# Splitting the second pair of each group's weight units one to three steps later in a fused attention and mixture-of-experts kernel

## The chip, the cores and the metric

The kernel runs on one core of a Trainium2 chip. The metric is device time in microseconds (us) for one launch, as the median of several runs; a single profiled execution gives the trace. Engines are named as the profile does: PE is TensorE (the matrix unit), PEld its weight loads, DVE VectorE, ACT ScalarE, POOL GpSimd, and SP is SyncE, which here issues all DMA transfers.

## The reference, cut to what matters

```
# attention, batch 4, heads 8, sequence 576, head size 64
scores = q @ k.T / 8 + (cum[:, None] - cum[None, :])   # cum = cumsum(log f)
scores = where(causal, -1e9, scores)
x = softmax(scores) @ v                   # reshaped to 2304 tokens x 512
# four experts over all tokens, hidden size 1024
p = probs / (probs.sum(-1) + 1e-9)
for e in range(4):
    out += p[:, e] * (maximum(x @ w1[e], 0) @ w2[e])
```

## The kernel before, in words

Attention and experts are interleaved so that PE always has something to multiply. Tokens come in chunks of 256. The expert weights are cut into 32 *units* of 128 x 1024 (a unit is one 128-wide slice of the hidden size: half of it belongs to `w1`, half to `w2`), and the tokens are swept twice, so there are 64 units: 0 to 31 in the first sweep, 32 to 63 in the second. Before PE can use a unit, its fp32 values are *split* into a high and a low half of lower precision, and every product is made of three matmuls (high x high, high x low, low x high).

**A step** is one chunk of tokens with one pair of units. `l1` (L1012, 24 matmuls) makes the hidden values, `gate` makes their high part `gh` on ACT (L1025) and their low part `gl` on DVE (L1026), and `l2` (L1045, 12 matmuls) of the step before multiplies by the second weights; DVE then adds the result to the chunk's sum `acc` (L1072). Two pairs of units (`ps` 0 and 1) are one group; the steps of a group go over the same chunks with both pairs.

**A unit's split** is `w_split(n)`. `w_load` issues the load of the raw unit into a tile `wr` (L937, 512 KB; three buffers). In the second sweep one half of the columns is split by ACT (L979, high part) and DVE (L980, low part), the other by POOL (L971 scales in place), ACT (L974) and POOL again (L975). The result is a pair tile; even units take a slot of the tag `wh`, odd units one of `wl`, with six slots each, and a new unit waits until PE has last used the unit that had its slot. Two steps later SP stores the split unit to memory (`wd`, L988), since a last stage reads it again. When a pair has been used for the last time (`ends` says at which step), the main loop calls `w_split(w0 + 6)` and `w_split(w0 + 7)`, and then `first_units(w0)`.

**The last stage** combines two units at a time (Strassen's scheme) from about 613 us on. Its first tiles are made early: for `w0` in `EARLY = (54, 58)`, `first_units` calls `split_1`, which loads a raw half unit (L1182, `wr64_0`, into the same three `wr` buffers), loads stored units into `bw0` (L1197), has POOL form sums `wt0` (L1177, four instructions that read `wr64_0`) and ACT and POOL split those into `bs0` (L1204, L1208, L1209). Both `bw0` and `bs0` take slots of the tag `wh`. The tiles `bv` (L1239) are further reads of stored units.

**Attention** has its own tiles in between: `raw` is a loaded block of q and k, `q`, `kl`, `hi` (L563, L571, L577, POOL) and ACT's `hi` (L562) prepare it, PE makes the scores (L615), DVE and ACT the softmax (L629, L644), ACT and DVE its normalised halves `z` (L713, L714). SP turns `z` around by DMA transposes into `pt` (L723, three for one half of a head pair), and PE multiplies `pt` with `v` (L816, tile `o`). The names end in head pair, batch and half: `pt3_3_1_1` is batch 3, pair of heads 1, second half, and `z`, `kl`, `q` of that half are made for it.

**What sets the order.** The body writes its instructions in program order, and a scheduler with a model of the engines then fixes the order on each engine, with the program order as the priority. Slots of a tag are handed out in program order too. On SP this order is also that in which DMAs are issued: an issue that waits holds all issues behind it.

Of the kernel before, what the change touches and what calls it, by code (L numbers as in the profile page):

```python
# [25 lines left out]
SWEEPS = (  # L26
    ((0,), (0,), (0, 1), (0, 1, 2)),
    ((1, 2, 3, 4), (1, 2, 3, 4), (2, 3, 4), (3, 4)),
)
# [7 lines left out]
LAST = (5, 6, 7, 8)  # L37
EARLY = (54, 58)
AHEAD = 4
W_SLOT = (4, 6)  # L40
NEAR = 2
JOBS = ((0, 0), (1, 0), (2, 0), (3, 0), (0, 1), (1, 1), (2, 1), (3, 1))
# [36 lines left out]
def fused(ctx: ExitStack, tc: tile.TileContext, qk, v, f, probs, w, out):  # L79
# [110 lines left out]
    def at_step(n, f):  # L190
        later.setdefault(n, []).append(f)
# [47 lines left out]
    def behind(f):  # L239
        if prev is None:  # L240
            f()
            return
        with tc.issue_after(prev.last.ins):
            f()
# [32 lines left out]
    def w_peek(e, i):  # L277

        n, k = divmod(i, 2)
        t = pk_p.tile([128, 512], F32, tag="pk", name=f"pk{e}_{i}")  # L280
        nc.sync.dma_start(out=t, in_=w[8 * e + n, :, 512 * k : 512 * k + 512])
        at_step(
            step + 2,
            lambda: nc.vector.tensor_reduce(
                out=wmax[:, k, n, e : e + 1], in_=t, op=ALU.max, axis=AX.X, apply_absolute_value=True
            ),
        )
# [57 lines left out]
    def v_peek(i):  # L345

        t = xf_p.tile([128, 1024], F32, tag=f"xf{2 + i % 2}", name=f"vp{i}")
        flat = v.rearrange("b r p t h d -> (b r p t h d)").rearrange(
            "(n p f) -> n p f", n=NV, p=128
        )  # L350
        nc.sync.dma_start(out=t, in_=flat[i])

        def top():
            with tc.issue_after(prev.first.ins):
                nc.scalar.activation(
                    out=t,
                    in_=t,
                    func=AF.Abs,
                    scale=1 / 1024,
                    accum_out=vmax[:, i : i + 1],  # L360
                )

        at_step(step + 2, top)
# [570 lines left out]
    def w_load(n):  # L934
        if n < NS and n not in wraw:
            wraw[n] = wr_p.tile([128, 1024], F32, tag="wr", name=f"wr{n}")
            nc.sync.dma_start(out=wraw[n], in_=w[n % 32])  # L937
# [3 lines left out]
    def w_pair(name):  # L941
        t = w_p.tile([128, 2, 1024], F16, tag=("wh", "wl")[len(pairs) % 2], name=name)
        pairs.append(t)
        return t

    def w_split(n):
        w_load(n)
        r = wraw.pop(n)
        if n < 32:
            wh[n] = w_p.tile([128, 1024], F32R, tag="wh", name=f"wh{n}")  # L950
            wl[n] = w_p.tile([128, 1024], F32R, tag="wl", name=f"wl{n}")
            nc.scalar.activation(out=wh[n], in_=r, func=AF.Copy)  # L952
            eng = nc.vector if n in W_DVE else nc.gpsimd
            for a in (0, 512):
                z = a + 512
                eng.tensor_tensor(  # L956
                    out=wl[n][:, a:z],
                    in0=r[:, a:z],
                    in1=wh[n][:, a:z].bitcast(F32),
                    op=ALU.subtract,  # L960
                )
        else:
            e = n % 32 // 8
            assert ("w", e) in known
            t = w_pair(f"w{n}")
            wh[n], wl[n] = t[:, 0], t[:, 1]
            for k in range(2):
                c = slice(512 * k, 512 * k + 512)
                sc = wsc[:, e, k : k + 1]
                if k == 1:  # L970
                    nc.gpsimd.tensor_scalar(  # L971
                        out=r[:, c], in0=r[:, c], scalar1=sc, scalar2=None, op0=ALU.mult
                    )
                    nc.scalar.activation(out=wh[n][:, c], in_=r[:, c], func=AF.Copy)  # L974
                    nc.gpsimd.tensor_tensor(  # L975
                        out=wl[n][:, c], in0=r[:, c], in1=wh[n][:, c], op=ALU.subtract
                    )
                    continue
                nc.scalar.activation(out=wh[n][:, c], in_=r[:, c], func=AF.Copy, scale=sc)  # L979
                nc.vector.scalar_tensor_tensor(  # L980
                    out=wl[n][:, c],
                    in0=r[:, c],
                    scalar=sc,
                    in1=wh[n][:, c],
                    op0=ALU.mult,
                    op1=ALU.subtract,
                )
            at_step(step + 2, lambda: nc.sync.dma_start(out=wd[n - 32], in_=t))  # L988
        w_load(n + 1)
        w_load(n + 2)  # L990
        w_load(n + 3)
# [196 lines left out]
    def split_1(p):  # L1188
        if p >= 16:
            return ()  # L1190
        r = raw_half(p, 0)
        t, u = (
            w_p.tile([128, 2, 1024], F16, tag="wh", name=f"b{k}{p}") for k in ("w", "s")
        )
        one = t.rearrange("p n (s f) -> p n s f", s=2)
        for n in range(2):
            nc.sync.dma_start(out=one[:, n], in_=wd[2 * p + n][:, :, :512])  # L1197
        bw[p] = one, u.rearrange("p s (k f) -> p s k f", k=4)
        f = sums(f"wt{p}", r, SUMS)
        hi, lo = u[:, 0], u[:, 1]  # L1200

        def scale(a):
            x = f[:, a : a + 512]
            nc.scalar.activation(out=x, in_=x, func=AF.Copy, scale=wsc[:, p // 4, 0:1])  # L1204

        def part(a):
            x, h = f[:, a : a + 512], hi[:, a : a + 512]
            nc.scalar.activation(out=h, in_=x, func=AF.Copy)  # L1208
            nc.gpsimd.tensor_tensor(out=lo[:, a : a + 512], in0=x, in1=h, op=ALU.subtract)  # L1209

        return (
            lambda: scale(0),
            lambda: (part(0), scale(512)),
            lambda: part(512),
        )

    def first_units(w0):
        if w0 in EARLY:
            for f_ in split_1(EARLY.index(w0)):
                f_()  # L1220
# [322 lines left out]
    goals = sorted((max(n - LEAD, 1), cost[need[c]]) for c, n in first.items() if n > 0)  # L1543
    goals.append((len(steps) - AHEAD, cost[-1]))
    while goals:
# [17 lines left out]
    def startup():  # L1563
# [13 lines left out]
        for s in range(FIRST + 2):  # L1577
# [24 lines left out]
            if s >= 5 and s % 2 == 1:  # L1602
                heads[s - 4][0].fin()
            if s in W_SLOT:
                w_split(W_SLOT.index(s))

# [9 lines left out]
    j.begin(0)  # L1616
    for n in range(len(W_SLOT), 6):
        w_split(n)

    used = set()  # L1620
    for n in range(len(steps) + 1):
        step = n
        cur = steps[n] if n < len(steps) else None
        for f_ in later.pop(n, ()):
            behind(f_)
        for e, first_ in enumerate(PEEK):
            if 0 <= n - first_ < 16:
                w_peek(e, n - first_)
            if n == first_ + 17:
                a_, b_ = w_scale(e)  # L1630
                behind(a_)
                at_step(n + 3, b_)
        if 0 <= n - V_PEEK < NV:
            v_peek(n - V_PEEK)
        if n == V_PEEK + NV + 1:
            a_, b_ = v_scale()
            behind(a_)
            at_step(n + 2, b_)
        if cur is not None:
            if cur.c not in used:  # L1640
                used.add(cur.c)
                upto(need[cur.c])
            for c, m in TURN:
                if n >= m and c not in yh and ("x", c) in known:
                    narrow(c)
            if cur.s == 1:
                assert cur.c in yh
                weigh(cur.g // 2, cur.c)
            for q in range(4):
                cur.l1(q)  # L1650
                pace(n + q / 8)
            cur.gate()
        else:
            upto(len(asteps))
            chunks.close()
            late.h = late.enter_context(tc.tile_pool(name="h", bufs=4, side="right"))
            for e in range(E):
                weigh(e, LAST[0])
            big = [Big(p) for p in range(16)]
            turns = in_turns(0)  # L1660
            for _ in range(3):
                next(turns)()
        if prev is not None:
            for q in range(4):
                prev.l2(q)
                pace(n + (q + 4) / 8)
                if cur is None:
                    for _ in range(2 if q == 3 else 1):
                        next(turns)()
            for w0, t in ends.items():  # L1670
                if t is prev:
                    if w0 + 7 < NS:
                        w_split(w0 + 6)
                        w_split(w0 + 7)
                    first_units(w0)
        prev = cur

    for p in range(2):
# [88 lines left out]
```

## Time and profile before

| what | value |
| --- | --- |
| median of 3 runs | 942.64 us (941.62 to 944.03) |
| profiled execution: time, span | 939.25 us, 937.5 us |
| mean granted clock of TensorE | 0.985 of full speed |
| busy: PE, DVE, ACT, POOL | 885.3, 709.3, 568.9, 525.1 us |
| moved by DMA | 159.45 MB, mean 170 GB/s |

The profiled execution is 3.39 us (0.4%) below the median of the runs. Its span is the time from its first instruction to its last, and 1.75 us lie around it. All times in the trace count from the span's start.

### The profile page before, as it was taken

Reading aid. Unit: us, or ns where it says so; the run is one execution under the profiler, and the core shown is the slowest. Engines: PE = TensorE matmul, PEld = TensorE weight load, DVE = VectorE, ACT = ScalarE, POOL = GpSimd, SP = SyncE. Lnnn points to the kernel's source line nnn. Section 1 sums busy time; section 2 is a strip of 40 time slices with the busy share of each in tenths; the row PEclk is TensorE's granted clock in tenths of the full one; section 3 lists DMA queues with packets and bytes.
Section 4 is the critical chain, followed back from the end, with each engine's and each line's share of the span. In section 5 each row is a group of like instructions: output and inputs, shape, how many; then the busy total and the mean of one; then the engine's idle time right before and its main releaser. Section 6 shows DMA issues by size and latency. Waiting matters only on the chain. (4 is left out here: it accounts for less than half of the span.)

```text
span 937.5 us, 16657 instructions
## 1 busy us (share of the span) xinstructions
PE 885.3 (94%) x5783; PEld 620.8 (66%) x5783; DVE 709.3 (76%) x1458; ACT 568.9 (61%) x1137; POOL 525.1 (56%) x528
## 2 busy tenths in 40 slices
PE   4899998999998889999999989999998999999998
PEld 3699988999765556666666656654455664666547
DVE  5768665786888988789878887576778757786487
ACT  5869755465676778668666777355665345653350
POOL 4657865478533754327641684265778627785060
PEclk9999999999998988999999999999999999999999
DMA  7458844538879698988999699524322424232003
GB/s 264 146 176 295 291 126 164 186 119 313 227 189 198 152 293 195 311 156 212 306 288 158 119 328 236 135 67 142 129 91 81 145 68 125 79 107 74 23 1 91
DMA packets 147508, 159.45 MB, mean 170 GB/s; under 512 B 86148, under 2 KB 107328, under 8 KB 147424
## 3 DMA queue, kind: packets, MB, share of 16 engines
q1 hardware_dynamic: 147424, 158.39, 60.2%
q8 instruction: 45, 0.74, 0.3%
q14 instruction: 39, 0.32, 0.2%
HBM read 117.30 MB, written 21.65 MB: 148 GB/s over the span
## 5 line engine op out<-in xcount | busy, mean ns | idle before, releaser
L1012 PE MATMUL l<-y,w 128*128 128x256 f16 x1248 | 155.7, 275 | 0.0
L1012 PEld LDWEIGHTS <-w 128*128 128x128 f16 x1248 | 118.3, 99 | 30.6 <-issue 6.5
L644 ACT ACTIVATE p<-p,nm 128x576 f32<-128x576 f32 (+3 forms) x160 | 95.6, 598 | 52.4 <-DVE nm L629 43.5
L1045 PE MATMUL l<-w,gh 128*128 128x512 f16 x408 | 122.6, 383 | 4.8 <-DVE acc L1072 4.8
L714 DVE SCALAR_TENSOR_TENSOR z<-p,rs,z 128x384 f16<-128x384 f32 (+3 forms) x128 | 85.7, 694 | 12.6 <-ACT z L713 11.1
L1072 DVE SCALAR_TENSOR_TENSOR acc<-y,scg,acc 128x256 f32<-128x256 f32 (+1 forms) x164 | 81.1, 515 | 14.9 <-PE y L1283 14.7
L615 PE MATMUL s<-hi 128*128 128x384 f32 (+1 forms) x192 | 76.9, 406 | 16.1 <-DVE hi L577 8.9
L563 POOL CAST q<-raw 64x320 fp32r<-64x320 f32 (+1 forms) x56 | 26.0, 465 | 117.9 <-PE s L615 71.3
L1283 PE MATMUL m<-rh,bs 128*128 128x512 f16 x256 | 86.4, 379 | 0.0
L629 DVE CUSTOM_DVE_ANT_0 p<-s,mask 128x288 f32<-128x288 f32 (+2 forms) x160 | 74.8, 475 | 12.9 <-PE s L615 11.8
L571 POOL TENSOR_TENSOR kl<-raw,hi 64x576 fp32r<-64x576 f32 (+1 forms) x56 | 66.4, 1186 | 28.6 <-ACT hi L562 28.2
L1045 PE MATMUL l<-w,gl 128*128 128x512 f16 x204 | 77.1, 383 | 5.0 <-DVE gl L1026 5.0
L1209 POOL TENSOR_TENSOR bs<-wt,bs 128x512 f16<-128x512 f32 x32 | 38.4, 1201 | 75.7 <-ACT bs L1208 75.4
L971 POOL TENSOR_SCALAR wr<-wr,wsc 128x512 f32<-128x512 f32 x32 | 53.9, 1687 | 35.1 <-DMA wr<-in_w 25.5
L956 POOL TENSOR_TENSOR wl<-wr,wh 128x512 fp32r<-128x512 f32 x48 | 64.4, 1370 | 15.9 <-ACT wh L952 11.6
L713 ACT ACTIVATE z<-p,rs 128x384 f16<-128x384 f32 (+3 forms) x128 | 69.5, 589 | 4.6 <-issue 1.2
L1026 DVE SCALAR_TENSOR_TENSOR gl<-l,gh 128x512 f16<-128x512 f32 (+1 forms) x80 | 54.7, 684 | 19.1 <-ACT gh L1025 18.6
L1012 PE MATMUL l<-xh,wh 128*128 128x256 f32 x224 | 65.0, 292 | 0.8 <-ACT xh L857 0.8
L615 PE MATMUL s<-kl,q 66*128 66x384 f32 (+1 forms) x192 | 63.7, 336 | 2.2 <-DMA kl<-nc 2.2
L1283 PE MATMUL m<-rh,bw 128*128 128x512 f16 x191 | 64.4, 379 | 1.4 <-ACT r L1329 1.4
L1012 PE MATMUL l<-xl,wh 128*128 128x256 f32 x224 | 65.2, 291 | 0.0
L1045 PEld LDWEIGHTS <-gh 128*128 128x128 f16 x408 | 37.0, 98 | 42.2 <-issue 11.2
(387 smaller groups left out, 2359.6 us busy)
## 6 DMA issues: line engine op xcount, KB each, us to landing
wr<-in_w SPq DMA_DIRECT2D x90, 512.0 KB
pk<-in_w SPq DMA_DIRECT2D x64, 256.0 KB
wd<-w SPq DMA_DIRECT2D x32, 512.0 KB
raw<-in_qk SPq DMA_DIRECT2D x32, 448.0 KB
bw<-wd SPq DMA_DIRECT2D x32, 256.0 KB
bv<-wd SPq DMA_DIRECT2D x32, 256.0 KB
raw<-in_qk SPq DMA_DIRECT2D x24, 256.0 KB
vp<-in_v SPq DMA_DIRECT2D x10, 512.0 KB
```

The source lines that it names most:

```text
L571: eng.tensor_tensor(out=kl[:64, :wk], in0=r[:64, ko : ko + wk], in1=hi[:64, ko : ko + wk].bitcast(F32), op=ALU.subtract,)
L615: nc.tensor.matmul(out=ps[:, at : at + z - a], lhsT=lhsT, rhs=rhs, start=(m == 0), stop=(m == 1),)
L629: nc.vector.tensor_tensor_reduce(out=pt[:, a:z], in0=ps, in1=mask[:, m0 + a : m0 + z], scale=-0.125, scalar=BIG if n == 0 else nm[:, col : ...
L644: nc.scalar.activation(out=pt[:, :w_], in_=pt[:, :w_], func=AF.Exp, scale=-1.0, bias=self.nmax[hh][:, c : c + 1], accum_out=self.ssum[:, h ...
L713: nc.scalar.activation(out=o[:, 0], in_=x, func=AF.Copy, scale=sc)
L714: nc.vector.scalar_tensor_tensor(out=o[:, 1], in0=x, scalar=sc, in1=o[:, 0], op0=ALU.mult, op1=ALU.subtract)
L956: eng.tensor_tensor(out=wl[n][:, a:z], in0=r[:, a:z], in1=wh[n][:, a:z].bitcast(F32), op=ALU.subtract,)
L1012: nc.tensor.matmul(out=self.l1p[:, fi, :], lhsT=lhsT, rhs=rhs[:, k, :], start=(k == 0 and m == 0), stop=(k == 3 and m == 2),)
L1026: self.last = nc.vector.scalar_tensor_tensor(out=self.gl, in0=self.l1p, scalar=0.0, in1=self.gh.bitcast(F32) if wide else self.gh, op0=ALU ...
L1045: matmul(out=l2[tt], lhsT=lhsT, rhs=rhs, start=(self.ps == 0 and fi == 0 and m == 0), stop=(self.ps == 1 and fi == 1 and m == 2),)
L1072: nc.vector.scalar_tensor_tensor(out=acc[c][:, tt, d0:d1], in0=ps, scalar=sc, in1=acc[c][:, tt, d0:d1], op0=ALU.mult, op1=ALU.add,)
L1283: line.append(nc.tensor.matmul(**args))
```

## The change

`REST`, indexed by the number of chunks that a group's steps go over, gives a delay in steps: none for one chunk, 1, 2 and 3 steps for two, three and four chunks. For the second pair of a group (`ps` = 1) the two `w_split` calls no longer come at the end of that pair's last step, but `REST[...]` steps later; they are kept in `splits` and called at the end of the loop body, behind `first_units`.

```diff
--- before.py
+++ after.py
@@ -37,6 +37,7 @@
 LAST = (5, 6, 7, 8)
 EARLY = (54, 58)
 AHEAD = 4
+REST = (0, 0, 1, 2, 3)
 W_SLOT = (4, 6)
 NEAR = 2
 JOBS = ((0, 0), (1, 0), (2, 0), (3, 0), (0, 1), (1, 1), (2, 1), (3, 1))
@@ -1617,7 +1618,7 @@
     for n in range(len(W_SLOT), 6):
         w_split(n)
 
-    used = set()
+    used, splits = set(), {}
     for n in range(len(steps) + 1):
         step = n
         cur = steps[n] if n < len(steps) else None
@@ -1670,9 +1671,11 @@
             for w0, t in ends.items():
                 if t is prev:
                     if w0 + 7 < NS:
-                        w_split(w0 + 6)
-                        w_split(w0 + 7)
+                        wait = REST[len(SWEEPS[t.s][t.g // 2])] if t.ps else 0
+                        splits.setdefault(n + wait, []).extend((w0 + 6, w0 + 7))
                     first_units(w0)
+            for m in splits.pop(n, ()):
+                w_split(m)
         prev = cur
 
     for p in range(2):
```

Nine pairs move in the program: units 24 and 25 and units 28 and 29 by one step; 32, 33 and 36, 37 by two; 44, 45 and 48, 49 and 52, 53 by three; 56, 57 and 60, 61 by two. The pairs in between stay where they are.

In the order on the engines, eight of the nine moves show nothing but two places at which SP issues a store and a load the other way round. The ninth, units 60 and 61, changes the order between about 525 and 600 us of the trace of before: `first_units(54)` now comes ahead of these units in the program, so that `bw0` and `bs0` take the two `wh` slots that come free first, and unit 60 gets a later one, that of unit 52. Its raw tile `wr60` keeps one of the three `wr` buffers meanwhile.

**On SP**, before, the load of unit 63 (`wr63`) and the store of unit 60 (`wd28`) stood ahead of the transposes into `pt3_2_1_0` and of `wr64_0`:

```order
L937 DMA wr62_7579<-in_w 128x1024
L988 DMA wd27_161<-w59_7573 128x2048
L937 DMA wr63_7685<-in_w 128x1024
L988 DMA wd28_162<-w60_7679 128x2048
L1085 DMA out_0<-acc2_3037 128x512
L723 DMA_TRANSPOSE pt3_2_1_0_7236<-z0_3053 128x6x128
L723 DMA_TRANSPOSE pt3_2_1_0_7236<-z0_3053 128x8x128
L723 DMA_TRANSPOSE pt3_2_1_0_7236<-z2_3055 128x9x64
L1085 DMA out_0<-acc2_3037 128x512
L1182 DMA wr64_0_7693<-in_w 128x2x512
L988 DMA wd29_163<-w61_7687 128x2048
```

and further on, between the transposes into `pt3_3_1_0` and `pt3_3_1_1`, stood only these (`bv0`, `bv1` read stored units, `wd30` stores unit 62):

```order
L723 DMA_TRANSPOSE pt3_3_1_0_7503<-z0_3053 128x6x128
L1239 DMA bv0_8266<-wd0_134 128x2x512
L723 DMA_TRANSPOSE pt3_3_1_0_7503<-z0_3053 128x8x128
L723 DMA_TRANSPOSE pt3_3_1_0_7503<-z2_3055 128x9x64
L1239 DMA bv0_8266<-wd1_135 128x2x512
L1239 DMA bv1_8269<-wd2_136 128x2x512
L1239 DMA bv1_8269<-wd3_137 128x2x512
L988 DMA wd30_164<-w62_7956 128x2048
L1182 DMA wr66_1_8304<-in_w 128x2x512
L723 DMA_TRANSPOSE pt3_3_1_1_7667<-z1_3054 128x6x128
L723 DMA_TRANSPOSE pt3_3_1_1_7667<-z1_3054 128x8x128
L723 DMA_TRANSPOSE pt3_3_1_1_7667<-z3_3056 128x9x64
```

Now `wr63` and `wd28` stand far behind:

```order
L1183 DMA wr64_0_7679<-in_w 128x2x512
L989 DMA wd29_163<-w61_7887 128x2048
L724 DMA_TRANSPOSE pt3_2_1_1_7397<-z1_3054 128x6x128
L724 DMA_TRANSPOSE pt3_2_1_1_7397<-z1_3054 128x8x128
L724 DMA_TRANSPOSE pt3_2_1_1_7397<-z3_3056 128x9x64
L938 DMA wr63_7885<-in_w 128x1024
L724 DMA_TRANSPOSE pt3_3_1_0_7503<-z0_3053 128x6x128
L724 DMA_TRANSPOSE pt3_3_1_0_7503<-z0_3053 128x8x128
L724 DMA_TRANSPOSE pt3_3_1_0_7503<-z2_3055 128x9x64
L989 DMA wd28_162<-w60_7879 128x2048
```

and between `wd28` and `pt3_3_1_1` stand nine transfers, two of them (`wr65_0`, and `wd31`, the store of unit 63) from before `pt3_2_1_1`, one (`wr66_0`) from before `pt3_3_1_0`:

```order
L1183 DMA wr65_0_8015<-in_w 128x2x512
L989 DMA wd31_165<-w63_7960 128x2048
L1240 DMA bv0_8266<-wd0_134 128x2x512
L1240 DMA bv0_8266<-wd1_135 128x2x512
L1183 DMA wr66_0_8283<-in_w 128x2x512
L1240 DMA bv1_8269<-wd2_136 128x2x512
L1240 DMA bv1_8269<-wd3_137 128x2x512
L989 DMA wd30_164<-w62_7954 128x2048
L1183 DMA wr66_1_8304<-in_w 128x2x512
L724 DMA_TRANSPOSE pt3_3_1_1_7667<-z1_3054 128x6x128
L724 DMA_TRANSPOSE pt3_3_1_1_7667<-z1_3054 128x8x128
L724 DMA_TRANSPOSE pt3_3_1_1_7667<-z3_3056 128x9x64
```

The issue of `wd28` waits for the instructions of DVE (L981 of the changed kernel) and of POOL (L976) on unit 60; that of `wr63` waits for POOL's last read of `wr64_0`.

**On POOL**, before, unit 63 and the preparation of attention's last half (`q2_1`, `kl3_3_1_1`, `hi3_3_1_1`) came ahead of the sums `wt0`:

```order
L971 TENSOR_SCALAR wr62_7579<-wr62_7579,wsc_122 128x512
L971 TENSOR_SCALAR wr63_7685<-wr63_7685,wsc_122 128x512
L563 CAST q2_1_117<-raw3_3_1_1_7259 64x320
L975 TENSOR_TENSOR w63_7962<-wr63_7685,w63_7962 128x512
L571 TENSOR_TENSOR kl3_3_1_1_7257<-raw3_3_1_1_7259,hi3_3_1_1_7420 64x576
L577 TENSOR_TENSOR hi3_3_1_1_7420<-raw3_3_1_1_7259,hi3_3_1_1_7420 64x320
L1177 TENSOR_TENSOR wt0_7699<-wr64_0_7693 128x256 x2
L1177 TENSOR_TENSOR wt0_7699<-wt0_7699,wr64_0_7693 128x256
L1177 TENSOR_TENSOR wt0_7699<-wr64_0_7693,wt0_7699 128x256
L1209 TENSOR_TENSOR bs0_7696<-wt0_7699,bs0_7696 128x512 x2
L975 TENSOR_TENSOR w62_7956<-wr62_7579,w62_7956 128x512
```

Now the sums stand ahead of and between these, and units 60 and 63 behind them all:

```order
L972 TENSOR_SCALAR wr62_7579<-wr62_7579,wsc_122 128x512
L1178 TENSOR_TENSOR wt0_7685<-wr64_0_7679 128x256 x2
L564 CAST q2_1_117<-raw3_3_1_1_7243 64x320
L1178 TENSOR_TENSOR wt0_7685<-wt0_7685,wr64_0_7679 128x256
L572 TENSOR_TENSOR kl3_3_1_1_7241<-raw3_3_1_1_7243,hi3_3_1_1_7418 64x576
L578 TENSOR_TENSOR hi3_3_1_1_7418<-raw3_3_1_1_7243,hi3_3_1_1_7418 64x320
L1178 TENSOR_TENSOR wt0_7685<-wr64_0_7679,wt0_7685 128x256
L1210 TENSOR_TENSOR bs0_7682<-wt0_7685,bs0_7682 128x512 x2
L972 TENSOR_SCALAR wr63_7885<-wr63_7885,wsc_122 128x512
L976 TENSOR_TENSOR w60_7879<-wr60_7317,w60_7879 128x512
L976 TENSOR_TENSOR w63_7960<-wr63_7885,w63_7960 128x512
L976 TENSOR_TENSOR w62_7954<-wr62_7579,w62_7954 128x512
```

**On DVE**, before, the split of unit 60 and a softmax instruction stood ahead of `gl1_5_2_1` (the low part of step (5, 2, second pair)):

```order
L980 SCALAR_TENSOR_TENSOR w60_7679<-wr60_7176,wsc_122,w60_7679 128x512
L714 SCALAR_TENSOR_TENSOR z1_3054<-p3_1_1_1_2_6939,rs3_1_1_6834,z1_3054 128x3x128
L714 SCALAR_TENSOR_TENSOR z1_3054<-p3_1_1_1_3_6940,rs3_1_1_6834,z1_3054 128x4x128
L714 SCALAR_TENSOR_TENSOR z3_3056<-p3_1_1_1_4_6941,rs3_1_1_6834,z3_3056 64x4x128
L714 SCALAR_TENSOR_TENSOR z3_3056<-p3_1_1_1_4_6941,rs3_1_1_6834,z3_3056 64x64
L629 ISA p3_2_1_0_4_7128,nm3_2_1_0_7129<-s3_2_1_0_4_0_7225,mask_115 128x288
L629 ISA nm3_2_1_0_7129 128x1
L1026 SCALAR_TENSOR_TENSOR gl1_5_2_1_7211<-l1_1_5_2_1_7180,gh1_5_2_1_7210 128x512
```

Now neither does:

```order
L715 SCALAR_TENSOR_TENSOR z1_3054<-p3_1_1_1_2_6937,rs3_1_1_6816,z1_3054 128x3x128
L715 SCALAR_TENSOR_TENSOR z1_3054<-p3_1_1_1_3_6938,rs3_1_1_6816,z1_3054 128x4x128
L715 SCALAR_TENSOR_TENSOR z3_3056<-p3_1_1_1_4_6939,rs3_1_1_6816,z3_3056 64x4x128
L715 SCALAR_TENSOR_TENSOR z3_3056<-p3_1_1_1_4_6939,rs3_1_1_6816,z3_3056 64x64
L1027 SCALAR_TENSOR_TENSOR gl1_5_2_1_7195<-l1_1_5_2_1_7164,gh1_5_2_1_7194 128x512
L630 ISA p3_2_1_0_4_7128,nm3_2_1_0_7129<-s3_2_1_0_4_0_7209,mask_115 128x288
L630 ISA nm3_2_1_0_7129 128x1
L981 SCALAR_TENSOR_TENSOR w61_7887<-wr61_7571,wsc_122,w61_7887 128x512
```

A little further on DVE, `gl1_5_3_0` has moved from ahead of one `acc` and four `z` instructions to behind them.

## Rows read from the trace of the kernel before

**Rows 1.** The page, part 1: busy time, share of the span, instructions
```profile
PE 885.3 (94%) x5783; PEld 620.8 (66%) x5783; DVE 709.3 (76%) x1458; ACT 568.9 (61%) x1137; POOL 525.1 (56%) x528
```

**Rows 2.** What TensorE waited for, 500 to 600 us: total, times, longest
```profile
PE l L1045 <- DVE gl L1026: 2.1, 1, 2.1
PE l L1045 <- DVE acc L1072: 1.3, 1, 1.3
```

**Rows 3.** VectorE's timeline, 545 to 557 us: start, us, engine, line, operation, tiles
```profile
545.37 0.75 DVE L980 SCALAR_TENSOR_TENSOR w<-wr,wsc,w 128x512 f16<-128x512 f32 x1 [0.23 <-POOL hi L577]
...
549.89 0.46 DVE L629 CUSTOM_DVE_ANT_0 p<-s,mask 128x288 f32<-128x288 f32 x1
...
550.27 0.69 DVE L1026 SCALAR_TENSOR_TENSOR gl<-l,gh 128x512 f16<-128x512 f32 x1
...
554.74 0.69 DVE L1026 SCALAR_TENSOR_TENSOR gl<-l,gh 128x512 f16<-128x512 f32 x1
...
556.01 1.27 DVE L714 SCALAR_TENSOR_TENSOR z<-p,rs,z 128x384 f16<-128x384 f32 x2
```

**Rows 4.** TensorE's timeline, 558 to 594 us
```profile
558.83 0.38 PE L1045 MATMUL l<-w,gl 128*128 128x512 f16 x1
...
570.69 0.42 PE L615 MATMUL s<-hi 128*128 128x384 f32 x1
...
578.59 0.61 PE L1045 MATMUL l<-w,gh 128*128 128x512 f16 x2
...
593.97 1.69 PE L816 MATMUL o<-pt,v 128*64 128x320 f16 x27
```

**Rows 5.** GpSimd's timeline, 563 to 596 us; in brackets idle time and its releaser
```profile
563.82 1.40 POOL L571 TENSOR_TENSOR kl<-raw,hi 64x576 fp32r<-64x576 f32 x1
565.30 0.86 POOL L577 TENSOR_TENSOR hi<-raw,hi 64x320 fp32r<-64x320 f32 x1
568.80 1.41 POOL L1177 TENSOR_TENSOR wt<-wr 128x256 f32<-128x256 f32 x2 [2.64 <-issue]
...
582.07 1.16 POOL L975 TENSOR_TENSOR w<-wr,w 128x512 f16<-128x512 f32 x1 [1.46 <-ACT w L974]
595.74 1.27 POOL L1162 TENSOR_TENSOR rx<-xf,xf 128x512 f32<-128x512 f32 x1 [12.52 <-PE o L816]
```

**Rows 6.** ScalarE's timeline, 560 to 579 us
```profile
560.25 0.72 ACT L979 ACTIVATE w<-wr,wsc 128x512 f16<-128x512 f32 x1 [1.23 <-DMA wr<-in_w]
...
575.15 2.21 ACT L713 ACTIVATE z<-p,rs 128x384 f16<-128x384 f32 x4 [0.24 <-DVE rs L675]
```

**Rows 7.** SyncE's timeline of DMA issues, 552 to 588 us
```profile
552.58 0.56 SPq L937 DMA_DIRECT2D wr<-in_w  x1
553.19 1.17 SPq L988 DMA_DIRECT2D wd<-w  x1
...
556.64 5.70 SPq L723 DMA_TRANSPOSE pt<-z  x3
...
563.06 0.40 SPq L1182 DMA_DIRECT2D wr<-in_w  x1
...
564.54 1.14 SPq L988 DMA_DIRECT2D wd<-w  x1
...
572.79 1.30 SPq L1182 DMA_DIRECT2D wr<-in_w  x1
...
581.16 1.90 SPq L1239 DMA_DIRECT2D bv<-wd  x3
...
587.51 4.66 SPq L723 DMA_TRANSPOSE pt<-z  x3
```

**Rows 8.** The chain of waits near 537 us: start, us, what
```profile
536.69 4.51 DMA wr<-in_w
```

**Rows 9.** The DMA view, 540 to 600 us: GB/s in 40 equal slices
```profile
GB/s 410 418 410 426 397 382 361 244 121 257 412 404 393 170 151 273 180 229 403 412 302 168 13 305 231 131 235 185 186 227 343 347 245 72 177 70 0 0 0 0
```

**Rows 10.** What TensorE waited for, 280 to 290 us
```profile
PE o L816 <- DMA pt<-z: 4.0, 1, 4.0
```

## The prediction

> **What bounds the kernel now.** I read the page first: PE is busy 885.3 us of the span [rows 1], so almost anything that does not make PE wait costs nothing. The order on the engines says where to look: it changes only between about 525 and 600 us, so the sum is made there. In 500 to 600 us PE waits twice, 2.1 us for DVE's `gl` and 1.3 us for DVE's `acc` [rows 2]. So all that this stretch can give back is 3.4 us; what it can lose has to be found in the timelines of the other engines, which run ahead of PE by small margins.
>
> The margin that matters most: SP issues the last three transposes, `pt3_3_1_1`, from 587.51 on, and the issues take 4.66 us, until 592.17 [rows 7]; PE uses them in the 27 matmuls at 593.97 [rows 4], right behind its matmuls before, without waiting. They have landed at most 6.46 us after the first issue (593.97 - 587.51), so the margin is between nothing and a little. How a missed one looks, the same kernel shows at 284 us, where PE waits 4.0 us for transposes [rows 10].
>
> **The sum, part by part.**
>
> *The eight moves without effect on the order.* Same instructions, same order; the two swapped issues on SP are issues of about 0.4 us each and lie far from any wait of PE in [rows 2]. Nothing, and if one of them mattered, no more than such an issue, 0.4 us.
>
> *A. The wait for `gl`.* `gl1_5_2_1` starts on DVE at 550.27, behind unit 60's split (0.75 us) and a softmax instruction (0.46 us) [rows 3]. Both are now behind it. Neighbours overlap by about 0.08 us each, so it comes 0.67 + 0.38 = 1.05 us earlier, and PE's wait shrinks from 2.1 to about 1.1 us: -1.0. It cannot gain the whole 2.1: the `z` instructions ahead of it stay. The wait for `acc` stays too: it follows from `wr59`, issued at 536.69 and landing 4.51 us later [rows 8], which has moved nowhere.
>
> *B. The next `gl`.* `gl1_5_3_0` (554.74 before) now stands behind four `z` and one `acc`. Two `z` took 1.27 us [rows 3]; with the other two and the `acc` some 3.0 to 3.5 us, less the 0.7 us that A gives DVE here. It ends at about 554.74 + 0.69 + 2.5 = 557.9, up to 558.2, while PE, 1.0 us ahead by A, wants it at 558.83 - 1.0 = 557.8 [rows 4]. With the releasing step in between I take +0.9: what A gives is taken back (bounds 0 and +1.2).
>
> *C. POOL.* The sums `wt0` now stand ahead of attention's last preparation, and they wait for `wr64_0`. That is issued at 563.06, and the first sum starts at 568.80, 5.74 us later [rows 5, 7]. Ahead of it on SP, `wr63` and the 1.17 us issue of unit 60's store are gone [rows 7], so it can be issued up to 2.4 us earlier (0.56 and 1.17 for these two issues, and 0.67 by which DVE delivers the `z` ahead of them sooner). Behind the landing POOL needs two sums (1.41), `q2_1` (a cast, about half a `hi`: 0.4), one more sum (0.7), `kl` (1.40) and `hi` (0.86) [rows 5]: 4.8 us, less overlaps 4.5. The scores that need them start on PE at 570.69 [rows 4]. With `wr64_0` landing 2.4 us earlier, at 566.4, they are ready at 570.9 and PE loses about 0.4 us with the hand-over; with no gain on SP, at 568.8, PE loses 2.6. I take 0.4, since SP's transposes there took 5.70 us for three [rows 7] while a backlog of loads ran that is now 1 MB smaller; bounds 0 and 2.6.
>
> *D. Unit 63 and unit 60.* `wr63` is issued after the last sum, at about 571.3, instead of 552.58 [rows 7], and lands 4.5 us later by [rows 8], at about 575.8. ACT's split of it (0.72 us [rows 6]) stands ahead of `gh` of step (5, 4, second pair). With `gh` (on ACT, no longer than that split) and `gl` (0.69 us on DVE [rows 3]) behind it this `gl` is ready at 577.9, and PE wants it just after 578.59 [rows 4]: hidden, by less than a microsecond. Then ACT makes four `z` (2.21 us [rows 6]) and a softmax piece, splits unit 60 in two instructions (three more at up to 0.72 each), and POOL does its last step on it (1.16 us, as for another unit in [rows 5]): unit 60 is done at about 582.7. In PE's order its first use stands behind the matmuls of 593.97, so nobody but SP waits for it.
>
> *E. SP.* But SP does. `wd28`, unit 60's store, now waits on SP until 582.7, and nine issues behind it wait too, ahead of `pt3_3_1_1`. The issues before took 1.17 (`wd28`), 0.40 (a raw half), 1.14 (`wd31`), 1.30 (`wr66_0`), four `bv` at 1.90/3 = 0.63, and two more at about 0.4 [rows 7]: 7.3 us, and with gaps of 0.09 us some 8. So `pt3_3_1_1` is issued from about 590.8 instead of 587.51: 3.3 us late. And ahead of it in the DMA queue lie six transfers of 512 KB and four of 256 KB, 4.19 MB. With a backlog the DMA moves 382 to 426 GB/s [rows 9]; at 410 that is 10.2 us. The first lands 4.5 us after issue, at 587.2, the last 9 us later, at 596.1, and the transposes behind it at 597 to 599.5; I take 598.7. PE reaches these matmuls at 593.97 - 1.0 + 0.9 + 0.4 = 594.3: it waits 4.4 us.
>
> Do transfers really wait for those issued ahead? `wr63` shows it: issued at 552.58 behind other loads and stores, it reached ACT at 560.25 [rows 6], 7.7 us later, against 4.51 us with an empty queue [rows 8]. The Trainium skill says the same of one queue (page "DMA: Bandwidth & Descriptors", section "Two DMAs through the same engine are not ordered"): descriptors start in order, but are pipelined, so a later one may finish beside an earlier one. By the first half of that sentence the wait is 4.4 us; if the pipelining lets the transposes finish beside the last loads, it would be some 1.3 us less, which is one 512 KB transfer. The same page (section "Where 436 GB/s comes from") puts a load from memory at about 358 GB/s. By that the 4.19 MB would take 11.7 us, and the sum would be 1.5 us more; the slices at 382 to 426 in [rows 9] differ from it, and the rows decide.
>
> Bounds of E: 0, if each issue takes no longer than the shortest of its kind, unit 60 is done near 580, and the transposes land within 6.46 us of the issue whatever lies ahead; and +7.5, if C's full 2.6 us pass on to unit 60, and SP's issues are held up by the backlog as they were at 556.64, where three took 5.70 us [rows 7].
>
> *The end.* PE does nothing else while it waits, and the last stage hangs on the attention output: POOL's `rx` at 595.74 had waited 12.52 us for these very matmuls [rows 5]. So a delay here passes through to the end.
>
> Sum: -1.0 + 0.9 + 0.4 + 4.4 = **+4.7 us**. Against the profiled execution's 939.25 that is 943.95; that execution is 3.39 us below the median of the runs, so for the median 942.64 + 4.7 = **947.3 us**. A measurement of this kernel tells about 0.3%, 2.8 us, from no change, so +4.7 counts as slower.
>
> **The rivals.**
>
> 1. *No change* (within 0.3%; 28%). E costs 0 to 2.8: POOL finishes unit 60 a little earlier, the `bv` and `wr` issues are short, or the transposes overtake loads. For it: E is a difference of two times that I estimate to within some 3 us, and the queue is never seen with exactly this load. Against it: 4.19 MB in 11 us of issue-to-need is what the DMA can do at its best, with no room for the transposes. Time: 942 to 945, likeliest 943.5 (A and B cancel, C 0.4, E about 0.5).
>
> 2. *Faster* (7%). A's mechanism without B and E: DVE is freed of unit 60's split just where PE waits for DVE, both waits of [rows 2] may shrink as the split moves into a slack stretch, and SP releases unit 60's store in time. It needs the store's issue before about 578, so that the backlog is gone before the transposes. Price: -1.0 for A, at most -3.4 with both waits; 939.2 to 941.6. Against it: `wr59`, which sets the wait for `acc`, does not move, and unit 60 waits behind unit 63's late load.
>
> 3. *A larger loss* (20% of the 65% for slower). C's late `wr64_0` holds POOL, PE loses up to 2.6 us at 570.69, and the `z` of the last half come later too, so E remains whole: +4.7 + 2.2 to +4.7 + 4; 949.5 to 951.5. For it: the margins in C and D are under 1 us.
>
> 4. *The change does nothing where it says so*, in eight of nine pairs. That is in the sum already.
>
> **How the numbers follow.** Slower 0.65 (45 at the forecast, 20 at the larger loss), same 0.28, faster 0.07. The range reaches from 941.5, which takes in most of the case of no change, to 951.5, the larger loss. For the likeliest case alone I would say 945.5 to 949.5.
>
> **What would show it.** Right: in the chain or PE's waits of the changed kernel a wait for `DMA pt<-z` of 3 to 6 us at about 594 to 600 us on PE's L816; the store of unit 60 issued by SP at about 581 to 585, with the transposes of `pt3_3_1_1` after 589; the wait for `gl` at 551 shrunk to about 1 us. Wrong: no such wait (then the queue let the transposes through, or unit 60 was done before 580), a new wait on PE's scores near 571 (then C was the larger), or a difference that stems from outside 525 to 600 us.

## The result and the profile after

Over twenty runs of each kernel the median went from 940.4 to 946.2 us; the ratio is 1.0061 with a 95% interval of 1.0048 to 1.0073, so the change costs 5.7 us (4.5 to 6.9). Forecast was +4.7 us. (The median of the kernel before is 940.4 here and was 942.64 over three runs; the forecast of 947.3 stood on the latter, and as a difference is what can be compared.) The profiled execution of the changed kernel has a span of 944.4 us, against 937.5.

What TensorE waited for in the same stretch as [rows 2], 500 to 610 us, changed kernel:

```profile
PE o L817 <- DMA pt<-z: 5.4, 1, 5.4
PE l L1046 <- DVE gl L1027: 1.9, 2, 1.1
PE l L1046 <- DVE acc L1073: 1.5, 2, 1.1
```

There is one large new wait, 5.4 us for transposes, and it is where the forecast put it: at the 27 matmuls that stood at 593.97 without a wait before [rows 4]. Its place on TensorE's timeline, changed kernel (start, us, instruction; in brackets the idle time and what ended it):

```profile
548.87 0.39 PE L1046 MATMUL l<-w,gl 128*128 128x512 f16 x1 [0.74 <-DVE gl L1027]
...
557.82 0.39 PE L1046 MATMUL l<-w,gl 128*128 128x512 f16 x1 [1.12 <-DVE gl L1027]
```

```profile
584.05 0.59 PE L1046 MATMUL l<-w,gh 128*128 128x512 f16 x2 [0.43 <-DVE acc L1073]
...
592.21 2.13 PE L1013 MATMUL l<-y,w 128*128 128x256 f16 x18
599.78 3.17 PE L817 MATMUL o<-pt,v 128*64 128x320 f16 x27 [5.44 <-DMA pt<-z]
```

The wait for `gl` near 551 us fell from 2.14 us (the 2.1 of [rows 2]) to 0.74, that for `acc` at 541 us from 1.32 to 1.05; a wait of 1.12 came at the next `gl`, and one of 0.43 for `acc` at 584.05. And the 27 matmuls took 3.17 us instead of 1.69. That they did is the clock, shown by the stretches of the changed kernel below (columns: busy time of PE, PEld, DVE, ACT, POOL with instruction counts, then the granted clock of TensorE, the DMA share and GB/s):

```profile
592.00:594.00 2.00, 2.00 (x19) 1.70 (x18) 0.89 (x2) 0.00 (x0) 0.00 (x0) 1.00 1.06 380
596.00:598.00 2.00, 0.00 (x0) 0.00 (x0) 0.00 (x0) 0.00 (x0) 0.00 (x0) 1.00 1.24 167
...
600.00:602.00 2.00, 2.00 (x18) 1.59 (x16) 0.00 (x0) 0.00 (x0) 0.00 (x0) 0.50 0.00 0
```

TensorE ran at the full clock (1.00, 2.4 GHz) before it stopped, had it still while it stood (596 to 598 us), and was at 0.50 (1.2 GHz) in 600 to 602 us when it went on; the kernel before has 1.00 in that stretch. So the wait cost 5.44 us and, in addition, 3.17 - 1.69 = 1.48 us.

That `bw0` now takes a slot ahead of unit 60 shows in its loads, which come 12.6 us earlier. Before, then changed:

```profile
541.37 1.67 SPq L1197 DMA_DIRECT2D bw<-wd  x2
528.73 1.22 SPq L1198 DMA_DIRECT2D bw<-wd  x2
```

The cause on SyncE, changed kernel, against [rows 7]:

```profile
559.90 0.40 SPq L1183 DMA_DIRECT2D wr<-in_w  x1
...
570.56 0.34 SPq L938 DMA_DIRECT2D wr<-in_w  x1
...
582.80 0.32 SPq L989 DMA_DIRECT2D wd<-w  x1
583.18 0.42 SPq L1183 DMA_DIRECT2D wr<-in_w  x1
583.70 0.88 SPq L989 DMA_DIRECT2D wd<-w  x1
584.67 1.98 SPq L1240 DMA_DIRECT2D bv<-wd  x2
586.70 0.63 SPq L1183 DMA_DIRECT2D wr<-in_w  x1
587.43 1.18 SPq L1240 DMA_DIRECT2D bv<-wd  x2
588.72 0.53 SPq L989 DMA_DIRECT2D wd<-w  x1
589.30 1.04 SPq L1183 DMA_DIRECT2D wr<-in_w  x1
590.43 7.27 SPq L724 DMA_TRANSPOSE pt<-z  x3
```

Unit 63's raw load is issued at 570.56 instead of 552.58, unit 60's store at 582.80 instead of 553.19, and behind it nine transfers; the transposes start at 590.43 instead of 587.51. What they carry is ready a little later too. VectorE, changed kernel, and under it the last half's `z` of the kernel before:

```profile
581.19 1.55 DVE L981 SCALAR_TENSOR_TENSOR w<-wr,wsc,w 128x512 f16<-128x512 f32 x1
...
588.41 2.35 DVE L715 SCALAR_TENSOR_TENSOR z<-p,rs,z 128x384 f16<-128x384 f32 x4
```

```profile
586.86 2.35 DVE L714 SCALAR_TENSOR_TENSOR z<-p,rs,z 128x384 f16<-128x384 f32 x4
```

The row at 581.19 is unit 60's split, which before stood at 545.37 [rows 3], and the last half's `z` follow at 588.41 (586.86 before). In TensorE's own time, the `z` began 7.1 us ahead of the need before (593.97 - 586.86) and 5.9 us now (the need is 599.78 - 5.44 = 594.34).

So the 5.44 us split into three, each the difference of two rows: the `z` have lost 7.11 - 5.93 = 1.18 us of their lead; from their start to the first issue it takes 590.43 - 588.41 = 2.02 us instead of 0.65, which is 1.37 more; and from the first issue to the matmuls 599.78 - 590.43 = 9.35 us instead of at most 6.46, which is 2.89 more. The first is the engines, the middle one the blocked issues, the last the queue. Of the last, 2.61 us show on SyncE: the three issues themselves take 7.27 us instead of 4.66 [rows 7]. From the end of the last issue to the matmuls it is 599.78 - 597.70 = 2.08 us, and was at most 593.97 - 592.17 = 1.80.

What the transposes waited for in the queue can be read from the sizes of the packets that the DMA moves. In the kernel before, from 588.5 to 593.5 us, SyncE issues nothing but these three transposes, and nearly all packets are under 512 bytes:

```profile
DMA packets 2507, 0.67 MB, mean 134 GB/s; under 512 B 2476, under 2 KB 2476, under 8 KB 2507
```

The changed kernel, from 590.4 to 595 us and from 595 to 599.5 us:

```profile
DMA packets 997, 1.62 MB, mean 351 GB/s; under 512 B 65, under 2 KB 599, under 8 KB 997
DMA packets 2665, 0.99 MB, mean 219 GB/s; under 512 B 2483, under 2 KB 2483, under 8 KB 2665
```

Read so, next to nothing of the transposes moves in the 4.6 us behind their first issue, while 1.62 MB of the transfers ahead do; then all of it moves in 4.5 us, where it took 5 before. The transposes start late behind the backlog, and their own transfer is not slowed.

The queue's rate, changed kernel, 580 to 604 us in 40 slices of 0.6 us:

```profile
GB/s 70 207 203 24 149 92 362 362 181 150 232 324 396 423 367 384 381 384 247 248 323 367 423 420 410 391 321 131 53 284 284 182 0 0 0 0 0 0 0 0
```

Between 588 and 595 us most slices lie between 323 and 423 GB/s, and by 600 us nothing moves. The rate that the Trainium skill gives for loads from memory (page "DMA: Bandwidth & Descriptors", section "Where 436 GB/s comes from"), about 358 GB/s, is passed in 13 of the 40 slices, which reach up to 423; stores and loads run together here, and the rows decide.

### The profile page after: what moved, and what is told of

Its sections match the earlier page's. It is cut to its first block, busy times and chain, and to the rows that moved or that the text cites. A ratio compares the mean times of both kernels' runs of the same rounds, so it can differ in the third digit from the quotient of the medians.

```text
span 944.4 us, 16660 instructions
## 1 busy us (share of the span) xinstructions
PE 886.2 (94%) x5783; PEld 621.7 (66%) x5783; DVE 711.0 (75%) x1458; ACT 569.2 (60%) x1137; POOL 525.1 (56%) x528
## 4 chain that ended last, share of the span: by engine, by line
PE 48%; POOL 14%; DVE 12%; DMA 7%; ACT 7%; issue 6%; SPq 1%; POOLq 0%; DVEq 0%; ACTq 0%
PE l L1013 14%; PE l L1046 14%; PE y L1284 6%; PE m L1284 5%; POOL s L1344 5%; POOL wt L1178 4%; DMA wr<-in_w 3%; PE s L616 3%; DVE z L715 2%; POOL wu L1178 2%; PE o L817 2%; DMA pt<-z 2%; DVE acc L1073 1%; DVE p L630 1%; DMA wd<-w 1%
```

## The experiments

The theory was that the loss comes from the move of units 60 and 61 alone, and there from three transposes that are issued behind a blocked store and a long queue. The rivals were that the eight other moves carry some of it, that the delay as such does it, and that the transposes are late because their data are. The edits below are shortened; each is against the changed kernel where no other is named.

**Which part of the change: the eight other pairs.**

```diff
 if w0 + 7 < NS:
-    wait = REST[len(SWEEPS[t.s][t.g // 2])] if t.ps else 0
-    splits.setdefault(n + wait, []).extend((w0 + 6, w0 + 7))
+    if w0 == 54:
+        w_split(60); w_split(61)
+    else:
+        wait = REST[len(SWEEPS[t.s][t.g // 2])] if t.ps else 0
+        splits.setdefault(n + wait, []).extend((w0 + 6, w0 + 7))
```

> The eight other pairs are moved as in the change; units 60 and 61 stay where they were before. If the loss comes from units 60 and 61 alone (my theory): within 0.2% of before, no wait of TensorE for transposes near 594 us, the waits for gl and acc near 541 to 551 us as before (2.1 and 1.3 us). Rival, that the eight moves carry part of the loss: 1 to 6 us above before.

Measured: ratio 1.0010 (0.9982 to 1.0039). TensorE's waits from 500 to 610 us in this kernel:

```profile
PE l L1046 <- DVE gl L1027: 2.1, 1, 2.1
PE l L1046 <- DVE acc L1073: 1.4, 1, 1.4
```

These are the waits of before, and there is none for transposes. Eight of the nine moves change nothing that can be measured; by the interval they cost at most 0.4%, 3.7 us.

**Units 60 and 61 alone.**

```diff
-    wait = REST[len(SWEEPS[t.s][t.g // 2])] if t.ps else 0
-    splits.setdefault(n + wait, []).extend((w0 + 6, w0 + 7))
+    if w0 == 54:
+        splits.setdefault(n + 2, []).extend((60, 61))
+    else:
+        w_split(w0 + 6); w_split(w0 + 7)
```

> Only units 60 and 61 are moved, by two steps, and so come behind the early tiles of the last stage. My theory: the whole loss, 4.5 to 7 us above before, with a wait of TensorE of 4.5 to 6 us for transposes at about 594 to 600 us. Rival, that the eight other moves carry part of it: less than 4 us above before.

Measured: ratio 1.0100 (1.0063 to 1.0138), so at least the whole loss.

```profile
PE o L817 <- DMA pt<-z: 5.2, 1, 5.2
```

The same wait for transposes, 5.2 us. The ratio's middle is above the change's own 1.0061, but the intervals meet.

**The place in the program without the delay.** Here units 60 and 61 are split in the old step, but written behind the early tiles of the last stage (the edit is against the kernel before):

```diff
 if w0 == 54:
+    first_units(w0)
     w_split(w0 + 6)
     w_split(w0 + 7)
-    first_units(w0)
```

> Units 60 and 61 are split in the same step as before, only written behind the early tiles of the last stage instead of ahead of them; nothing is delayed by steps. If the place behind the early tiles is the cause: the same as only60, 4.5 to 7 us above before, with the same wait for transposes. Rival, that the delay of two steps is the cause: within 0.2% of before.

Measured: ratio 1.0088 (1.0057 to 1.0119), and in the trace

```profile
PE o L817 <- DMA pt<-z: 5.4, 1, 5.4
```

With no step of delay the loss is all there, and the order on POOL, ACT, DVE and PE is the same as in the changed kernel. So the loss needs no delay. The change also puts the calls behind `first_units`, and what costs is that the early tiles `bw0` and `bs0` then come first in program order and take the slots that unit 60 would have had: `bw0` is loaded at 527.68 us here, as early as in the changed kernel, and at 539.75 where only the eight other pairs move.

**The delay without the place.** All nine pairs are delayed as in the change, and `first_units(54)` is delayed too, so that it comes behind units 60 and 61 again:

```diff
-    first_units(w0)
+    if w0 == 54:
+        units = n + 2
+    else:
+        first_units(w0)
 ...
 for m in splits.pop(n, ()):
     w_split(m)
+if n == units:
+    first_units(54)
```

> All nine pairs are delayed as in the change, and the early tiles of the last stage, written two steps later as well, come behind units 60 and 61 again. If the place behind the early tiles is the cause and not the delay: unit 60's store is issued near 553 us as before, no wait for transposes near 594 us, and a time within 0.5% of before (the early tiles come later, which may cost or give up to 3 us in the last stage). Rival, that the delay is the cause: 4.5 to 7 us above before with the wait for transposes.

Measured: ratio 1.0185 (1.0138 to 1.0232), far outside what was expected. The half about unit 60 holds: SyncE of this kernel issues its store early (the row after `wr63`'s), and TensorE does not wait for transposes:

```profile
552.33 0.38 SPq L938 DMA_DIRECT2D wr<-in_w  x1
552.77 1.19 SPq L989 DMA_DIRECT2D wd<-w  x1
```

But TensorE now waits in the last stage. The longest of its waits from 580 to 660 us is for the early tile `bs0`, which is late; the next two are for `rh` and `rl`, which ScalarE and VectorE make there from the tokens, and for which the kernel before does not wait:

```profile
PE m L1284 <- ACT bs L1209: 5.8, 1, 5.8
PE m L1286 <- ACT rh L1164: 2.2, 1, 2.2
PE m L1284 <- DVE rl L1165: 1.7, 1, 1.7
```

and its clock, in the stretches of the same kernel, is at half:

```profile
611.00:615.00 4.00, 3.62 (x9) 1.28 (x9) 4.00 (x4) 1.85 (x3) 3.71 (x3) 0.50 0.00 0
616.00:622.00 6.00, 0.23 (x1) 0.00 (x0) 3.25 (x3) 3.33 (x6) 5.92 (x6) 0.50 0.09 23
622.00:624.00 2.00, 1.97 (x8) 1.08 (x9) 1.28 (x2) 2.00 (x4) 2.00 (x2) 0.50 0.97 341
```

So "early" for these tiles is not to be given away either: 5.8, 2.2 and 1.7 us of waits, and matmuls at 0.50 of the clock from 611 to 624 us. Of the orders that were run, only the old one serves both the unit's split and the early tiles.

**The queue, first half: the stores.** The changed kernel with the stores of units 60, 62 and 63 put behind the last transposes:

```diff
-at_step(step + 2, lambda: nc.sync.dma_start(out=wd[n - 32], in_=t))
+def store():
+    with tc.issue_after(turned[-1].ins) if n in (60, 62, 63) else nullcontext():
+        nc.sync.dma_start(out=wd[n - 32], in_=t)
+at_step(79 if n in (60, 62, 63) else step + 2, store)
```

> The changed kernel, but with the stores of units 60, 62 and 63 issued behind the last three transposes; the loads ahead of these (2.6 MB) and all work on the engines keep their order. Queue theory (late issue behind a blocked store, and a backlog of 4.2 MB): the wait for transposes falls from 5.4 us to between 0 and 1.5 us, the time to within 0.3% of before. Rival (the softmax output of the last half is itself late, by 1.5 us on VectorE, and the queue does not matter): the wait stays at 5 us and the time at 4.5 to 7 us above before.

Measured: ratio 1.0053 (1.0031 to 1.0074). SyncE and TensorE of this kernel:

```profile
580.41 0.39 SPq L1191 DMA_DIRECT2D wr<-in_w  x1
...
586.66 5.23 SPq L727 DMA_TRANSPOSE pt<-z  x3
```

```profile
594.03 1.69 PE L820 MATMUL o<-pt,v 128*64 128x320 f16 x27 [2.75 <-DMA pt<-z]
```

The wait fell from 5.44 to 2.75 us and the 27 matmuls take 1.69 us again, but the wait is not gone as expected. By the split used above, with this kernel's `z` at 586.01: 1.8 us for later `z`, nothing for blocked issues (586.66 - 586.01 = 0.65), and 594.03 - 586.66 = 7.37 against 6.46 for the queue, 0.9 us. I had left the late `z` out. (They count for more here than the 1.2 us above, since TensorE comes to these 27 matmuls sooner: 12 matmuls stand ahead of them, 1.47 us, and not the 18 of 2.13 us.) The time is less clear than the trace. Its interval meets that of the changed kernel; the ten runs spread from 939.3 to 949.8 and the profiled one is the fastest of them; from the `acc` wait at 541 us to 596 us it loses 2.4 us against before.

**The queue, second half: the loads.** The changed kernel with `bv0` and `bv1` (1.05 MB) behind the last transposes:

```diff
 for p in range(2):
-    split_2(p)
+    with tc.issue_after(turned[-1].ins):
+        split_2(p)
```

> The changed kernel, but with four loads of 256 KB (1.05 MB, tiles bv0 and bv1) issued behind the last three transposes. If the backlog sets the wait: its transfer time of 1.05 MB at 0.41 MB per us is 2.6 us, and the wait of 5.4 us falls to 2 to 3.5 us, the time by 2 to 3.5 us. If the late issue alone sets it: at most 1.5 us are gained, as the issues of these four take 3.2 us but the transposes cannot be issued before about 589 us instead of 590.4. If late data sets it: no gain.

Measured: ratio 1.0043 (1.0023 to 1.0062); the wait is

```profile
600.17 3.17 PE L819 MATMUL o<-pt,v 128*64 128x320 f16 x27 [3.72 <-DMA pt<-z]
```

with the first issue at 592.49 and `z` at 591.80: 7.68 us from issue to matmul instead of 9.35. So 1.7 us came out of the queue's part and 1.3 out of that of the issues; but the `z` came another 1.3 us later in this kernel, so that 3.72 us remain, and the matmuls behind this wait ran at half clock again (3.17 us). The backlog's share is confirmed in sign and, at 1.7 of 2.6 us expected, roughly in size. This rests on the trace: the interval of the time meets that of the changed kernel.

**Both.** Stores and `bv` loads behind the last transposes; only three raw loads stay ahead.

> The changed kernel with both held back behind the last three transposes: the stores of units 60, 62 and 63 and the four bv loads; only three loads (1.57 MB) stay ahead. In the runs with one of the two held back, the wait that is left splits into transposes that land later after their first issue (1.2 and 0.9 us more than before) and z of the last half that comes 1.8 to 2.5 us later against TensorE than before. If that is right, the queue's share is gone here and a wait of 1.2 to 2.5 us stays, set by the late z; time 1 to 3 us above before. If the rest was still the backlog: no wait, time as before.

Measured: ratio 1.0016 (0.9992 to 1.0040).

```profile
594.83 1.69 PE L820 MATMUL o<-pt,v 128*64 128x320 f16 x27 [1.12 <-DMA pt<-z]
```

```profile
589.11 3.90 SPq L727 DMA_TRANSPOSE pt<-z  x3
```

The wait is down to 1.12 us; the loss cannot be told from nothing any more, and its interval lies below the changed kernel's (1.0048 to 1.0073). From the first issue to the matmuls it is 594.83 - 589.11 = 5.72 us, less than the 6.46 of before; what is left is the late `z`. All instructions of the engines but a few of TensorE are in the order of the changed kernel here, so the engines' order costs about 1 us, and what stands on SyncE ahead of the transposes the rest.

**More of it on the kernel before.** Nothing moved, but four needless stores of 512 KB just ahead of the last transposes (an addition to what is computed, nothing left out):

```diff
 def store():
     nc.sync.dma_start(out=wd[n - 32], in_=t)
+    if n == 62:
+        for x in spare:          # four tiles in memory that nobody reads
+            nc.sync.dma_start(out=x, in_=t)
```

> The kernel before with four more stores of 512 KB (unit 62 to memory that nobody reads) issued just ahead of the last three transposes; no unit is moved. This adds 2.1 MB, 5.1 us of transfer, and next to no issue delay. If transposes wait in the queue behind what was issued ahead: a new wait of TensorE for transposes of 3.5 to 5.5 us near 594 us and a time 3 to 6 us above before. If transposes pass large transfers, or there is more room than I think: less than 1 us of wait and a time within 0.2% of before.

Measured: ratio 1.0064 (1.0039 to 1.0088): the time came out, the place did not. The scheduler put other matmuls ahead of those 27: 56 of `l1`, where 36 stood between them and the one `o` matmul before them. SyncE and TensorE of this kernel:

```profile
589.16 3.70 SPq L994 DMA_DIRECT2D sp<-w  x4
592.90 1.56 SPq L1190 DMA_DIRECT2D wr<-in_w  x1
594.56 5.71 SPq L724 DMA_TRANSPOSE pt<-z  x3
```

```profile
603.63 1.72 PE L817 MATMUL o<-pt,v 128*64 128x320 f16 x27
```

TensorE no longer waits for transposes; but these matmuls come at 603.63 instead of 593.97. Half of this has nothing to do with the stores: in this profile, the slowest of the four runs, TensorE is already 4.9 us behind the kernel before at the one `o` matmul (590.03 against 585.10), and by as much since 558 us, ahead of their first issue at 589.16. The rest is theirs, and the last stage, which hangs on their result, is late in turn:

```profile
PE m L1291 <- ACT rh L1171: 2.6, 1, 2.6
PE m L1291 <- DVE rl L1172: 1.7, 1, 1.7
```

From the one `o` matmul to the end this profile loses 9.6 - 4.9 = 4.7 us. This says more than the experiment was made for. TensorE's wait is only where the delay shows; filling it with other work did not win it back here. That transposes queue behind stores is not shown by it alone, as the issues came late as well.

**The raw buffers.** The changed kernel, with unit 63's raw load asked for ahead of the early tiles:

```diff
+if w0 == 54:
+    w_load(63)
 first_units(w0)
```

> The changed kernel, but unit 63's raw load is asked for ahead of the early tiles, so that it comes ahead of wr64_0 again, and with it unit 63's split and store; unit 60 stays late. If the order of the raw buffers made the loss: no wait for transposes, time within 0.3% of before. If unit 60's late slot and its store in front of the transposes make it: with 2.6 MB behind that store in place of 4.2 a wait of 2 to 4.5 us stays, and the time is 2 to 6 us above before.

Measured: ratio 1.0114 (1.0068 to 1.0159), worse than either case. Unit 60 holds one of the three raw buffers until it is split. The next load now is unit 63's, it can be issued at 561.65 only, and ScalarE's and VectorE's split of unit 63 stand ahead of the softmax. ScalarE of this kernel:

```profile
566.33 0.72 ACT L980 ACTIVATE w<-wr,wsc 128x512 f16<-128x512 f32 x1 [6.91 <-DMA wr<-in_w]
```

TensorE waits 5.8 us for `acc` and 3.5 for transposes in this kernel. In the changed kernel the same late buffer goes to `wr64_0`, and only POOL waits for it (7.63 us before the row at 564.45), where there is room. With the old order of unit 63's load and `wr64_0` a wait for transposes of 3.5 us stays, so that order did not make the loss; the buffer that unit 60 holds would, if something nearer to TensorE waited for it.

**A version meant to beat both.** The kernel before, with ScalarE's and VectorE's half of unit 59 put behind the `acc` for which TensorE waits at 541 us, and that of unit 60 behind `gl` at 551 us:

```diff
+with tc.issue_after(hold[n].ins) if n in hold else nullcontext():
     nc.scalar.activation(out=wh[n][:, c], in_=r[:, c], func=AF.Copy, scale=sc)
     nc.vector.scalar_tensor_tensor(...)
```

> The kernel before, with VectorE's and ScalarE's first half of unit 59 put behind the sum of step (4, 4, second pair) and that of unit 60 behind gl of step (5, 2, second pair): the two waits of TensorE at 541 and 551 us (1.3 and 2.1 us) without any move in the program. If those waits are set by these splits standing in front: the waits fall to below 0.5 and to about 0.5 us, and the time by 1.5 to 2.8 us below before. Rival (the waits are set by the z instructions and the next one in the row takes their place): less than 0.8 us gained.

Measured: ratio 0.9992 (0.9975 to 1.0009), no gain that can be told. The waits of this kernel:

```profile
PE l L1048 <- DVE gl L1027: 2.0, 1, 2.0
PE l L1048 <- ACT gh L1026: 0.6, 1, 0.6
```

The one for `acc` is gone, that for `gl` is still 2.0 us: TensorE arrives sooner, and the same `z` instructions (544.84 to 548.5) stand ahead of `gl` at 548.95 on VectorE. No version that was run is faster than the kernel before.

## Why the prediction was right

The forecast of +4.7 us lies within the interval (4.5 to 6.9), with the likeliest case as the one that happened.

- *The eight moves at nothing*: shown, 1.0010 (0.9982 to 1.0039).
- *A, -1.0*: the wait for `gl` lost 1.4 us. *B, +0.9*: 1.12. Together nothing, as forecast.
- *C, +0.4*: TensorE did not wait at all. `wr64_0` was issued at 559.90, even earlier than the 560.7 that was the better bound.
- *D*: `wr63` at 570.56 (forecast 571.3); hidden, but for 0.43 us of a wait for `acc`.
- *E, +4.4*: the store of unit 60 at 582.80 (582.7), the transposes at 590.43 (590.8), TensorE ready for them at 594.34 (594.3), the matmuls at 599.78 (598.7), the wait 5.44. The path held step by step. What was too small, by 1.0 us in the wait, is the time from the first issue to the matmuls: 9.35 us, where the sum has 598.7 - 590.8 = 7.9. The backlog was through about as forecast (the small packets move from 595 us on; forecast 596.1), but the transposes behind it took over 4 us, where the sum has 2.6. Besides, the `z` came 1.2 us late, which the sum left out; here SyncE was later still, but the version with a short queue shows that about 1 us of wait stays when SyncE's part is gone.
- *The clock*: the 1.48 us at half clock had no place in the sum. The kernel before could have told: behind the 4.0 us wait of [rows 10] its clock was 0.50 from 287 to 293 us.
- The 4.51 us of [rows 8], which the prediction takes for a landing with an empty queue, are not that: three transposes were issued just ahead, from 531.66 to 536.59. In the changed kernel `wr63`, issued at 570.56, is split by ScalarE at 574.31, at most 3.75 us later.
- *The end*: a delay there passes through; borne out by the version with more stores, where TensorE had other work and 4.7 us were lost all the same.
- The rival *larger loss* by way of POOL did not come: POOL's wait for `wr64_0` is in the trace (7.63 us) and nobody waits for POOL.

By rows of the two profiles the region loses -0.27 - 1.40 + 1.12 + 0.43 + 5.44 + 1.48 = 6.8 us (the first is the wait for `acc` at 541 us, 1.05 instead of 1.32), and the spans differ by 6.9. The sum of 4.7 is 2.1 short of that: 1.0 in E and 1.5 for the clock, less 0.4 elsewhere. The times of the twenty runs moved by only 5.7, and that the forecast lies within their interval is to this extent luck.

The prediction followed the new place and the slots, and did not ask whether the delay itself does anything. The title names the delay; the runs show that the place behind `first_units` makes the whole loss without it, and that eight delays without that place cost nothing measurable. That the delay of units 60 and 61 would be harmless by itself is not shown by a time, since the version made for it lost more for another reason. What stays open: why the version with the stores held back took 5.0 us (2.9 to 7.0) in its runs where its profile loses 2.4; and what decides whether the clock falls behind a wait of 2 to 3 us.

## What to carry to other kernels

Where a scheduler sets the order by priorities and hands out slots in program order, a call that is moved is two changes: when it may run, and who comes before it in line for buffers. Compare the orders first; eight of nine moves here swapped two pairs of DMA issues and nothing else. When a load or store waits, look at what stands behind it on the same issuing queue, and count the bytes that will be let go at once ahead of a small transfer that the critical engine needs. And price a wait of TensorE with the clock behind it, not by its length alone.

## What was not expected of the hardware

After waits of 5.44 and 3.72 us the next matmuls were granted half the clock (0.50 and 0.51 in the 600 to 602 us of the two kernels; 27 matmuls in 3.17 us), after waits of 2.75 and 1.12 us the full clock (1.69 us). The length of the wait alone does not decide it. In the version with the `bv` loads held back a wait of 2.51 us, ended at 491.38, was followed by 0.50 (491 to 494 us); in that with more stores one of 2.14 us, ended at 554.30, also by 0.50 (555 to 557 us); and in the kernel before the wait of 2.14 us that ended at 551.02 was followed by 1.00 (552 to 554 us). In the version with the early tiles late, where TensorE stood for 2.2, 1.7 and 5.8 us between 607 and 622 us, the clock was 0.50 from 611 to 624 us.

SyncE's issues of transposes take longer when more is queued ahead: the last three took 3.90 us behind three loads, 5.23 with the stores held back, 5.71 with the `bv` loads held back, and 7.27 in the changed kernel.
